# One core, attention and two MoE layers: the small slot's stages put between another slot's products, a third buffer of attention values, the second slot's rows fetched in one step

## The chip, the cores and the metric

The kernel runs on one core of one Trainium2 chip. The metric is the device time of one execution in microseconds (us).

## The reference

```python
def _attn_ref(q, k, v, n_sink, window):
    scores = np.matmul(q, k.transpose(0, 1, 3, 2)) / np.sqrt(D)
    keep = is_sink | in_window
    scores = np.where(keep, scores, -1000000000.0)
    a = np.exp(scores - np.max(scores, axis=-1, keepdims=True))
    a = a / (np.sum(a, axis=-1, keepdims=True) + 1e-09)
    return np.matmul(a, v)

def _moe_ref(x, modality_id, w_gate, modality_bias, w1, w2):
    logits = x @ w_gate + modality_bias[modality_id]
    e_idx = np.argmax(logits, axis=1)
    ...
    for e in range(E):
        mask = e_idx == e
        h = np.maximum(x[mask] @ w1[e], 0.0)
        out[mask] = gate_w[mask, None] * (h @ w2[e])

def _moe2_ref(x, w_in, w_out):
    h = x @ w_in
    g = h * np.clip(h + 3.0, 0.0, 6.0) / 6.0
    return g @ w_out
```

Attention has 4 batches of 8 heads, 768 positions and head size 64; with 4 sink columns and a window of 128. Its output, 3072 tokens of 512, goes through a routed MoE (8 experts, top 1, hidden 1024), and that through a dense layer with a gate (hidden 2048), whose two weights arrive in 64 bits.

## The kernel before

The program is one long schedule, written out by hand: the order in the code is the order on each engine, and each engine (TensorE or PE, VectorE or DVE, ScalarE or ACT, GpSimd or POOL, SyncE or SP) works through its own instructions in that order, waiting for the others by semaphores. SP issues most loads; ACT issues some transfers too; POOL issues the indirect ones. An engine whose next instruction waits holds all that it has behind it.

**Attention** (to about 245 us). `attend(n)` (L1199) lists the pieces of head n beside those of heads n-1 to n-3. At an even n it first issues loads: keys and queries of the pair n+4 (`load_qk`, L204), the values of the pair n itself (`load_v`, L218, buffer `vt`, two buffers), the sink rows of the pair n+2. Those values are read first by `values_mm` (L341) two heads later. `scale_q` (L230) scales the next pair's queries on ACT.

**Routing** (`route`, L377) finds each token's expert; four batches, the last beside the first products of the MoE. Scaled rows go to DRAM (`xs_d`, from ACT, L483), token numbers are scattered into a table `tt_d` (POOL, L488).

**The routed MoE** works in slots (L1419). Slots 0 to 3 are 400 tokens each of the largest expert, slot `SMALL` = 4 holds 128 tokens of another expert with its own weights, slots 5 to 8 are 400 tokens each of the second largest. A slot's token numbers are asked for (`ask`, L1175, `ti`), its rows gathered in four indirect DMAs (`fetch`, `gather`, L718, `xg`), transposed (`slot_x`, L729), multiplied by w1 (`slot_h`, L749: 8 groups of 12 products, L758) and w2 (`slot_y`, L770: 8 half groups of 12, L779), and written (`slot_out`, L848: `yT_d`, `ids_d`, from ACT's queue). After each 12 products stands a `step()` (L1371), which issues what is due: a table `due` says which function runs in which step. A 400 slot has 16 steps, the small slot five. Steps also carry the splits of weights (`weight_split`, L681: ACT copies the high half, POOL or DVE subtracts; pace by `SPLITS`) and the narrowing of the last layer's weights (`narrow`, L866: 32 pieces, each loaded into `cv64`, converted in three sub-steps on ACT, DVE and POOL, stored as `w_d`; pace by `NARROWED`). A load of weights to be split goes into one of three `stg` buffers (`stage`, L670).

**The small slot** has five stages, one function each (L791 to L846): `small_x` transposes the rows, `small_h` makes 8 products of 128x512 per weight half and a ReLU on ACT into `hr`, `small_ht` transposes `hr`, `small_y` makes the second products, `small_yt` transposes back into `ys`. Its weights are used as they are, in fp32 (`raw`, L697; loaded 7 steps ahead by `load_small`, L1159). In the order on PE these stages follow one another between slot 3's last product and slot 5's first; only the transposes of slot 5's rows stand between them.

**The last layer** takes 12 tiles of 256 tokens (from about 585 us). A general path (L1450) for other inputs is in the program and is not entered with these.

The loop over the slots:

```python
for r in range(NS + 1):
    if r == SMALL:
        w = lambda i: W["small"][i]
        h = self.small_h(xT[r]["xT"], w, step)
        h = self.small_ht(h, step)
        y = self.small_y(h, w, step)
        when(pt, lambda y=y, r=r: self.slot_out(self.small_yt(y), tk[r], creg[r]))
    else:
        h = self.slot_h(xT[r]["xT"], weights(r), step)
        y = self.slot_y(h, weights(r), step)
        self.slot_out(y, tk[r], creg[r])
```

Of the kernel before, what the change touches and what calls it, by code (L numbers as in the profile page):

```python
# [54 lines left out]
class Net:  # L55
# [321 lines left out]
    def route(self, b):  # L377
# [107 lines left out]
        def sc(i):  # L485
            n = b * NB + i
            g.memset(self.rt.tile([P, 1], F32, name="apart"), 0.0)
            d = g.indirect_dma_start(out=self.tt, out_offset=IndirectOffsetOnAxis(r["si"][:, i:i + 1], 0),  # L488
                                     in_=self.toki[:, n:n + 1], in_offset=None)
            if not self.looped:  # L490
                self.scattered(d)
# [16 lines left out]
        return q  # L508

# [199 lines left out]
    def tokens(self, base, j=NJ, tp=TP, queue=None):  # L709

        ti = self.gp.tile([tp, j], I32, name=f"ti{j}", bufs=5 if j > 1 else 2)
        d = (queue or self.nc.sync).dma_start(
            out=ti, in_=self.tt[ds(base, j * tp), :].rearrange("(j p) o -> p (j o)", p=tp))
        if not self.looped:
            self.after_scatters(d)
        return ti

    def gather(self, ti, n=NT):  # L718
# [8 lines left out]
        return xg, [lambda i=i: rows(i) for i in range(j)]  # L727

# [62 lines left out]
    def small_x(self, xg):  # L791
# [11 lines left out]
        return r, [turn]  # L803

    def small_h(self, xT, w, side):

        nc = self.nc
        h = self.stg.tile([P, FF], F32, name="hr", tag="stg")
        for z in range(2):
            ph = self.mm.tile([P, 512], F32, name="mm")  # L810
            for k in range(4):
                nc.tensor.matmul(ph, xT[:, k], w(k)[:, z * 512:(z + 1) * 512], start=(k == 0), stop=(k == 3))
            nc.scalar.activation(h[:, z * 512:(z + 1) * 512], ph, AF.Relu)
            side()
        return h

    def small_ht(self, h, side):
        nc = self.nc
        hT = self.hp.tile([P, 8, P], F32, name="h")
        for z in range(2):  # L820
            t = self.mm.tile([P, 512], F32, name="mm").rearrange("p (i q) -> p i q", i=4)
            for i in range(4):
                nc.tensor.transpose(t[:, i], h[:, (4 * z + i) * P:(4 * z + i + 1) * P], self.ident)
            nc.scalar.copy(hT[:, 4 * z:4 * z + 4], t)
            side()
        return hT

    def small_y(self, hT, w, side):
        nc = self.nc
        py = self.mm.tile([P, 512], F32, name="mm")  # L830
        for f in range(8):
            nc.tensor.matmul(py, hT[:, f], w(4 + f // 2)[:, f % 2 * DM:(f % 2 + 1) * DM], start=(f == 0), stop=(f == 7))
            if f == 3:
                side()
        yr = self.yp.tile([P, DM], F32, name="y")
        nc.scalar.copy(yr, py)
        return yr

    def small_yt(self, yr):
        nc = self.nc  # L840
        t = self.pt.tile([P, 4, P], F32, name="tp")
        for d in range(4):
            nc.tensor.transpose(t[:, d], yr[:, d * P:(d + 1) * P], self.ident)
        y = self.stg.tile([P, 4, P], F32, name="ys", tag="stg")
        nc.scalar.copy(y, t)
        return y  # L846
# [19 lines left out]
    def narrow(self, pieces):  # L866
# [16 lines left out]
        def load(i):  # L883
            t = st["t", i] = self.cv.tile([P, 512, 2], I32, name="cv64", bufs=5)
# [28 lines left out]
        at = ((store, 8), (load, -8), (shift, 0), (size, 0), (sign, 1), (rest, 1), (small, 2), (whole, 3))  # L913
        q = [[(f, (k - d) // 3) for f, d in at if (k - d) % 3 == 0] for k in range(-8, 3 * n + 6)]
# [143 lines left out]
    def tile_out(self, g, wo, ids, side=None):  # L1058

        nc = self.nc  # L1060
        for t in range(T2 // P):
# [12 lines left out]
            else:  # L1074
                nc.scalar.copy(o, po)  # L1075
            nc.gpsimd.indirect_dma_start(out=self.out, out_offset=IndirectOffsetOnAxis(ids[:, t:t + 1], 0),  # L1076
# [3 lines left out]
    def build(self):  # L1080
        tc, nc = self.tc, self.nc
        with ExitStack() as ctx:
# [7 lines left out]
            self.w32 = dram.tile([16, P, 1024], F32, name="w32_d")  # L1090
            cp = pool("cp")
# [4 lines left out]
    def fast(self, cp):  # L1096
        tc, nc = self.tc, self.nc
        NBH = B * H
        with ExitStack() as ctx:
# [96 lines left out]
            def turns(s):  # L1196
                return self.small_x(xg[s]) if s == SMALL else self.slot_x(xg[s])

            def attend(n):  # L1199
# [6 lines left out]
                if a and n % 2 == 0:  # L1206
                    self.load_v(n)
# [31 lines left out]
            def scattered(b):  # L1239
# [17 lines left out]
                elif b == 2:  # L1257
                    slow.extend([lambda: self.first_slot(1)])
# [17 lines left out]
            with tc.manual_schedule(engines=COMPUTE):  # L1276
# [38 lines left out]
                def moved():  # L1315
# [3 lines left out]
                    self.cv = pool("cv", 1, cc, **right)  # L1319
                    narrow[:] = self.narrow(self.PIECES)  # L1320
# [22 lines left out]
                begin = [16 * r - 11 * (r > SMALL) for r in range(NS + 2)]  # L1343
# [289 lines left out]
```

## Time and profile before

| | |
|---|---|
| three runs | 1131.01, 1136.57, 1137.31 us; median 1136.57 us |
| the profiled execution | 1140.02 us; span of the profile 1138.2 us |
| granted TensorE clock, mean over the span | 0.986 |
| PE busy | 95% of the span |
| DVE, ACT, POOL busy | 42%, 40%, 23% |
| moved by DMA | 102.09 MB, 90 GB/s in the mean |
| chain that ended last, by engine | PE 78%, DMA 11%, DVE 4%, ACT 2% |

The timeline gives every operation with its start and length; in square brackets stands how long its engine had been idle, and whose work ended that. The span is 1.8 us shorter than the execution's own time, which is 3.5 us above the median of the three runs.

### The profile page before, as it was taken

How to read it: one execution, taken by the hardware profiler on the slowest of the kernel's cores; microseconds unless marked ns; L12 is line 12 of the kernel's file. 1: busy time of each engine (PE TensorE's matmuls, PEld its weight loads, DVE VectorE, ACT ScalarE, POOL GpSimd, SP SyncE). 2: the span in 40 equal slices, each digit the busy share in tenths (PEclk: the TensorE clock that was granted, in tenths of full speed). 3: DMA queues.
4: the chain of work that ended last, by engine and by line, in shares of the span. 5: the costliest groups of instructions: out<-in, count | busy, mean ns of one | idle time of the engine just before them, and what ended most of it. 6: DMA issues, size and time to landing. Idle time of an engine off the chain costs nothing.

```text
span 1138.2 us, 18251 instructions
## 1 busy us (share of the span) xinstructions
PE 1086.2 (95%) x6805; PEld 993.7 (87%) x6805; DVE 480.8 (42%) x1271; ACT 454.5 (40%) x1111; POOL 257.8 (23%) x458
## 2 busy tenths in 40 slices
PE   9999989897999979999999999999999999999995
PEld 6998878796999947999997989989989889899894
DVE  6666748655544414552243413314224134133140
ACT  4565636443355535652253413314224234143140
POOL 3433616445144324442031000000000000000000
PEclk9999989999999998999999999999999999999998
DMA  6343866514697795756332110100100101000000
GB/s 178 102 128 98 144 127 160 116 58 95 209 198 200 192 311 136 232 137 114 66 104 83 29 33 5 38 17 22 38 10 29 37 10 29 21 18 20 11 10 22
DMA packets 59891, 102.09 MB, mean 90 GB/s; under 512 B 17552, under 2 KB 34576, under 8 KB 59792
## 3 DMA queue, kind: packets, MB, share of 16 engines
q1 hardware_dynamic: 39966, 74.16, 25.3%
q10 hardware_dynamic: 13986, 13.53, 4.6%
q0 software_dynamic: 5840, 13.13, 4.5%
q8 instruction: 56, 0.92, 0.4%
q14 instruction: 43, 0.35, 0.1%
HBM read 72.87 MB, written 27.92 MB: 89 GB/s over the span
## 4 chain that ended last, share of the span: by engine, by line
PE 78%; DMA 11%; DVE 4%; ACT 2%; issue 1%; POOL 1%; SPq 1%; ACTq 0%; POOLq 0%; DVEq 0%
PE mm L1067 23%; PE mm L1045 22%; PE mm L779 10%; PE mm L758 9%; PE s L247 5%; PE o L354 2%; PE o L353 2%; DMA vt<-vv 2%; DMA yT_d<-y 1%; DMA xg<-xs_d,ti 1%; PE tp L318 1%; DMA ti<-tt_d 1%; DMA w<-w 1%; DMA stg<-w 1%; DMA ids_d<-ti 1%
## 5 line engine op out<-in xcount | busy, mean ns | idle before, releaser
L1045 PEld LDWEIGHTS mm<-yh,w 128*128 128x128 f32 x2304 | 274.6, 189 | 3.3 <-DVE u L1050 2.5
L1045 PE MATMUL mm<-yh,w 128*128 128x256 f32 x2304 | 275.1, 281 | 2.3 <-DVE u L1050 2.3
L1067 PE MATMUL mm<-w,ga 128*128 128x512 f32 x936 | 220.6, 394 | 0.1
L1067 PEld LDWEIGHTS mm<-w,ga 128*128 128x128 f32 x936 | 175.2, 188 | 39.9 <-DVE u L1050 0.3
L1048 ACT ACTIVATE r<-mm,b 128x256 f32<-128x256 f32 x192 | 91.2, 475 | 247.1 <-PE mm L1045 246.6
L779 PE MATMUL mm<-h,w 128*128 128x400 f32 x768 | 149.9, 350 | 3.2 <-DVE h L761 3.1
L758 PE MATMUL mm<-xT,w 128*128 128x400 f32 x768 | 143.5, 346 | 0.0
L779 PEld LDWEIGHTS mm<-h,w 128*128 128x128 f32 x768 | 139.4, 190 | 4.2 <-DVE h L761 4.2
L758 PEld LDWEIGHTS mm<-xT,w 128*128 128x128 f32 x768 | 139.8, 188 | 0.5 <-issue 0.5
L1050 DVE SCALAR_TENSOR_TENSOR u<-r,mm 128x256 f32<-128x256 f32 x192 | 80.8, 421 | 139.6 <-ACT r L1048 139.2
L1076 POOL DMA_INDIRECT out_dram<-ot,idt x24 | 23.1, 962 | 491.4 <-ACT ot L1075 368.9
L1073 DVE COPY ot<-mm 128x512 f32<-128x512 f32 x12 | 8.3, 692 | 222.0 <-PE mm L1067 222.0
L247 PE MATMUL s<-kz,qq 128*128 128x260 f32 (+1 forms) x384 | 95.6, 372 | 1.7 <-ACT qq L233 1.2
L283 ACT ACTIVATE pr<-s,mn 128x132 f32<-128x132 f32 x160 | 52.4, 370 | 75.8 <-DVE mn L272 40.5
L688 POOL TENSOR_TENSOR w<-stg,w 128x512 fp32r<-128x512 f32 x35 | 48.0, 1376 | 144.8 <-ACT w L686 134.1
L247 PEld LDWEIGHTS s<-kz,qq 128*128 128x128 f32 x384 | 62.5, 192 | 7.1 <-ACT qq L233 1.7
L761 DVE SCALAR_TENSOR_TENSOR h<-mm,h 128x400 fp32r<-128x400 f32 x64 | 36.5, 572 | 74.3 <-ACT h L760 73.2
L1035 DVE SCALAR_TENSOR_TENSOR ga<-u,ga 128x256 fp32r<-128x256 f32 x156 | 67.1, 430 | 0.0
L1034 ACT ACTIVATE ga<-u 128x256 fp32r<-128x256 f32 x156 | 63.8, 409 | 1.1 <-DVE u L1050 1.1
L354 PE MATMUL o<-vt,pt5p 128*128 128x66 f32 x320 | 62.6, 278 | 0.0
L353 PE MATMUL o<-vt,pt5d 128*128 128x66 f32 x320 | 61.4, 274 | 0.0
L336 POOL TENSOR_SCALAR_AFFINE_SELECT pt5d<-pt6a 128x256 f32<-128x256 f32 x64 | 30.5, 477 | 130.5 <-ACT pt6a L333 130.3
(228 smaller groups left out, 1249.8 us busy)
## 6 DMA issues: line engine op xcount, KB each, us to landing
stg<-w SPq DMA_DIRECT2D x16, 512.0 KB
cv<-w_in SPq DMA_DIRECT2D x16, 512.0 KB
w_d<-cva SPq DMA_DIRECT2D x32, 256.0 KB
cv<-w_out SPq DMA_DIRECT2D x16, 512.0 KB
stg<-w_d SPq DMA_DIRECT2D x16, 512.0 KB
yT_d<-y ACTq DMA_DIRECT2D x8, 800.0 KB
vt<-vv SPq DMA_DIRECT2D x16, 396.0 KB
kz<-kE SPq DMA_DIRECT2D x32, 197.0 KB
```

The lines of the kernel that those rows point to most:

```text
L247: nc.tensor.matmul(s[:, a, :n], q[:, b], k[:, c:c + n], start=True, stop=True)
L283: self.nc.scalar.activation(pr[:, i], s[:, a, P:P + W], AF.Exp, bias=mn[:, i:i + 1], scale=-1.0)
L353: mm(o[:, j], d[:, j - 1], vt[:, j], start=False, stop=False)
L354: mm(o[:, j], p[:, j - 1], vt[:, j - 1], start=False, stop=False)
L758: nc.tensor.matmul(ph[:, :T1], w(k)[:, wi, c], xT[:, xi, k], start=(n == 0), stop=(n == 11))
L779: nc.tensor.matmul(py[:, :T1], wf[:, wi], h[:, hi, f], start=(n == 0), stop=(n == 23))
L1034: nc.scalar.mul(g(0, f), u, 1.0 / 6.0)
L1035: nc.vector.scalar_tensor_tensor(g(1, f), u, 1.0 / 6.0, g(0, f).bitcast(F32), ALU.mult, ALU.subtract)
L1045: nc.tensor.matmul(ph[:, :T2], w, yh[:, b, k], start=(n == 0), stop=(n == 11))
L1048: nc.scalar.activation(r, ph[:, :T2], AF.Relu, bias=self.b3)
L1050: nc.vector.scalar_tensor_tensor(u, r, 6.0, ph[:, :T2], ALU.min, ALU.mult)
L1067: nc.tensor.matmul(po, g(a, f)[:, t * P:(t + 1) * P], w[:, b], start=(n == 0), stop=(n == 47))
```

## The change

- The five functions of the small slot become one, `small_slot`, which returns its stages by step number. They are due in steps 57 (in slot 3's second products) and 64 to 76 (in slot 5's). The small slot has no steps of its own any more, so that every later step number falls by five. `xs4`, `hT` and `ys` sit in the `stg` buffers, `hr` and `yr` in a new pool `sm` of one buffer.
- Slot 5's token numbers, rows and transposes come in steps 45, 48 and 59, all beside slot 3; before, in steps 50, 53 and 65, the transposes between the small slot's stages.
- To make room, `cv64` has four buffers instead of five, and a piece's load is listed five sub-steps ahead of its use instead of eight. The knots of `SPLITS` and `NARROWED` move with the step numbers.
- `vt` has three buffers; `attend(n)` issues the values of pair n+2 instead of those of pair n. At the start, the first pair's values and the small inputs are issued ahead of the second pair's keys and queries.
- Slot 1: its token numbers are asked for in attention's list (`scattered(2)`) right behind `first_slot(1)`, which runs at once; its four gathers are issued in one step instead of four.
- The general path has loops of single-row transfers in place of indirect DMAs (`spread`, `gather_rows`), with three new DRAM tensors. It is not entered here; its diff is left out.

```diff
-SPLITS = ((4, 0), (8, 8), (20, 8), (56, 16), (65, 16), (74, 24), (80, 24), (100, 32), (106, 32), (116, 40),
-          (126, 40), (133, 48), (134, 48), (148, 56))
-NARROWED = 105
+SPLITS = ((4, 0), (8, 8), (20, 8), (56, 16), (63, 16), (71, 24), (78, 24), (96, 32), (101, 32), (111, 40),
+          (121, 40), (128, 48), (129, 48), (143, 56))
+NARROWED = 100
...
-        vt = self.vp.tile([P, 2, NB, DV], F32, name="vt")
+        vt = self.vp.tile([P, 2, NB, DV], F32, name="vt", bufs=3)
...
-    def small_x(self, xg):
...
+    def small_slot(self, x, w, out):
...
         def turn():
             t = self.pt.tile([P, 4, P], F32, name="tp")
             for k in range(4):
-                nc.tensor.transpose(t[:, k], xg[:, 0, k * P:(k + 1) * P], self.ident)
-            r["xT"] = self.xtp.tile([P, 4, P], F32, name="xT")
+                nc.tensor.transpose(t[:, k], x()[:, 0, k * P:(k + 1) * P], self.ident)
+            r["xT"] = self.stg.tile([P, 4, P], F32, name="xs4", tag="stg")
             nc.scalar.copy(r["xT"], t)
...
+        def hidden(z):
+            if z == 0:
+                r["h"] = self.sm.tile([P, FF], F32, name="hr", tag="sm")
             ph = self.mm.tile([P, 512], F32, name="mm")
             for k in range(4):
...
+                nc.tensor.matmul(ph, r["xT"][:, k], w(k)[:, z * 512:(z + 1) * 512], start=(k == 0), stop=(k == 3))
+            nc.scalar.activation(r["h"][:, z * 512:(z + 1) * 512], ph, AF.Relu)
+
+        def turned(z):
+            if z == 0:
+                r["hT"] = self.stg.tile([P, 8, P], F32, name="hT", tag="stg")
             t = self.mm.tile([P, 512], F32, name="mm").rearrange("p (i q) -> p i q", i=4)
...
+        def outer(z):
+            if z == 0:
+                r["py"] = self.mm.tile([P, 512], F32, name="mm")
+            for f in range(4 * z, 4 * z + 4):
+                nc.tensor.matmul(r["py"], r["hT"][:, f], w(4 + f // 2)[:, f % 2 * DM:(f % 2 + 1) * DM],
+                                 start=(f == 0), stop=(f == 7))
...
+        def back():
...
+            out(y)
+
+        return {57: turn, 64: lambda: hidden(0), 65: lambda: hidden(1), 69: lambda: turned(0),
+                70: lambda: turned(1), 73: lambda: outer(0), 74: lambda: outer(1), 76: back}
...
-            t = st["t", i] = self.cv.tile([P, 512, 2], I32, name="cv64", bufs=5)
+            t = st["t", i] = self.cv.tile([P, 512, 2], I32, name="cv64", bufs=4)
...
-        at = ((store, 8), (load, -8), (shift, 0), (size, 0), (sign, 1), (rest, 1), (small, 2), (whole, 3))
+        at = ((store, 8), (load, -5), (shift, 0), (size, 0), (sign, 1), (rest, 1), (small, 2), (whole, 3))
...
-                if a and n % 2 == 0:
-                    self.load_v(n)
+                if n % 2 == 0 and n + 2 < NBH:
+                    self.load_v(n + 2)
...
-                    slow.extend([lambda: self.first_slot(1)])
+                    self.first_slot(1)
+                    slow.extend([None, None, lambda: ask(1)])
...
-                self.load_qk(2)
                 self.load_sink(0)
                 self.consts(cp, tmp)
                 ready = self.mask_kind(cp, tmp) + self.route_inputs(cp, tmp)
+                self.load_v(0)
+                self.load_qk(2)
...
-                begin = [16 * r - 11 * (r > SMALL) for r in range(NS + 2)]
+                begin = [16 * (r - (r > SMALL)) for r in range(NS + 2)]
...
-                        when(pt, *fetch(r))
-                    when(t - (1 if r == 1 else 3), lambda: ask(r))
+                        got = fetch(r)
+                        when(pt, *([lambda: [f() for f in got]] if r == 1 else got))
+                    if r != 1:
+                        when(t - 3, lambda: ask(r))
...
+                    if r > SMALL:
+                        b = begin[r] - 16
                     if r != 2:
-                        arrive(r, EARLY if r == 1 else begin[r - 2] + 5 if r == SMALL + 1 else b)
-                    turned(r, b + 1 if r == SMALL + 1 else b + 11)
+                        arrive(r, EARLY if r == 1 else b)
+                    if r != SMALL:
+                        turned(r, b + 11)
                 when(when_small, load_small)
+                ssteps = self.small_slot(lambda: xg[SMALL], lambda i: W["small"][i],
+                                         lambda y: self.slot_out(y, tk[SMALL], creg[SMALL]))
+                for t, f in ssteps.items():
+                    when(t, f)
```

What the compiled order shows at two places. A row is one engine's line, operation, output <- inputs and size, with a count where it repeats.

On PE, from slot 3's last products to slot 5's second; L779 and L758 are the 400 token slots' products, L812 and L832 the small slot's, L823 and L843 its transposes, L740 those of slot 5's rows. Before:

```order
L779 MATMUL mm<-h,w 128x400 x48
L812 MATMUL mm<-w,xT 128x512 x8
L740 MATMUL tp<-ident,xg 128x100 x4
L823 MATMUL mm<-ident,hr 128x128 x4
L740 MATMUL tp<-ident,xg 128x100 x4
L823 MATMUL mm<-ident,hr 128x128 x4
L740 MATMUL tp<-ident,xg 128x100 x4
L832 MATMUL mm<-w,h 128x512 x4
L740 MATMUL tp<-ident,xg 128x100 x4
L832 MATMUL mm<-w,h 128x512 x4
L758 MATMUL mm<-xT,w 128x400 x12
L843 MATMUL tp<-ident,y 128x128 x4
```

And now, where the same lines are L803, L782, L833, L848, L841 and L857:

```order
L803 MATMUL mm<-h,w 128x400 x12
L782 MATMUL mm<-xT,w 128x400 x12
L833 MATMUL mm<-w,xs_4913 128x512 x4
L782 MATMUL mm<-xT,w 128x400 x12
L833 MATMUL mm<-w,xs_4913 128x512 x4
L782 MATMUL mm<-xT,w 128x400 x48
L841 MATMUL mm<-ident,hr 128x128 x4
L782 MATMUL mm<-xT,w 128x400 x12
L841 MATMUL mm<-ident,hr 128x128 x4
L782 MATMUL mm<-xT,w 128x400 x12
L803 MATMUL mm<-h,w 128x400 x24
L848 MATMUL mm<-w,hT 128x512 x4
```

Between two stages of the small slot stand now 12 to 48 products of slot 5, where before there were four transposes or nothing.

On POOL, around the four gathers of slot 1's rows (L688 is a weight split's subtraction, L724 a gather, L487 and L488 belong to a scatter). Before:

```order
L688 TENSOR_TENSOR w<-stg,w 128x512 x4
L414 MEMSET r_ohz 128x8
L724 DMA xg<-xs_d,ti_3435 100x512
L688 TENSOR_TENSOR w<-stg,w 128x512
L724 DMA xg<-xs_d,ti_3435 100x512 x3
L487 MEMSET apart 128x1
L488 DMA tt_d<-toki,r_si 26624x1
```

And now, where L701 is the subtraction and L736 the gather:

```order
L701 TENSOR_TENSOR w<-stg,w 128x512 x4
L414 MEMSET r_ohz 128x8
L736 DMA xg<-xs_d,ti_3438 100x512 x4
L701 TENSOR_TENSOR w<-stg,w 128x512
L493 MEMSET apart 128x1
L494 DMA tt_d<-toki,r_si 26624x1
```

Three gathers moved ahead of one subtraction, and that subtraction behind them.

## Rows read from the trace of the kernel before

**Rows 1.** Page, part 1: TensorE (busy us, share, instructions)

```profile
PE 1086.2 (95%) x6805; PEld 993.7 (87%) x6805; DVE 480.8 (42%) x1271; ACT 454.5 (40%) x1111; POOL 257.8 (23%) x458
```

**Rows 2.** Timeline, SyncE queue, 138 to 145 us (start us, us, engine, line)

```profile
138.86 0.48 SPq L221 DMA_DIRECT2D vt<-vv  x1
```

**Rows 3.** Timeline, TensorE, 143 to 168 us ([idle before <- releaser])

```profile
143.77 0.71 PE L247 MATMUL s<-kz,qq 128*128 128x128 f32 x3
...
151.97 0.83 PE L247 MATMUL s<-kz,qq 128*128 128x128 f32 x4
...
159.78 0.62 PE L351 MATMUL o<-vt,pt6a 128*128 128x66 f32 x2 [5.33 <-DMA vt<-vv]
...
167.79 0.82 PE L247 MATMUL s<-kz,qq 128*128 128x128 f32 x4
```

**Rows 4.** Timeline, ScalarE, same stretch

```profile
157.59 0.84 ACT L233 ACTIVATE qq<-qq 128x768 f32<-128x768 f32 x1 [2.68 <-DMA qq<-qT]
```

**Rows 5.** Timeline, GpSimd, 263 to 273 us

```profile
267.87 1.27 POOL L688 TENSOR_TENSOR w<-stg,w 128x512 fp32r<-128x512 f32 x1 [0.62 <-ACT w L686]
...
270.67 1.00 POOL L724 DMA_INDIRECT xg<-xs_d,ti  x1 [0.30 <-issue]
271.97 1.00 POOL L724 DMA_INDIRECT xg<-xs_d,ti  x1 [0.30 <-issue]
```

**Rows 6.** Timeline, TensorE, 268 to 287 us

```profile
268.17 2.48 PE L779 MATMUL mm<-h,w 128*128 128x400 f32 x12
...
275.13 0.43 PE L740 MATMUL tp<-ident,xg 100*128 100x100 f32 x3
283.11 0.43 PE L740 MATMUL tp<-ident,xg 100*128 100x100 f32 x1 [7.54 <-DMA xg<-xs_d,ti]
283.24 3.73 PE L779 MATMUL mm<-h,w 128*128 128x400 f32 x12
```

**Rows 7.** Timeline, ScalarE and its queue, 271 to 285 us

```profile
271.16 0.33 ACTq L483 DMA_DIRECT2D xs_d<-xs  x1
...
283.95 0.72 ACT L476 ACTIVATE xs<-xb,r_gt 128x512 f32<-128x512 f32 x1 [7.81 <-DMA xs_d<-xs]
```

**Rows 8.** Stretches of 5 us: each engine busy, clock, DMA share, GB/s

```profile
275.00:280.00 5.00, 0.57 (x5) 0.36 (x3) 0.97 (x2) 0.72 (x1) 4.23 (x9) 0.93 1.00 178
```

**Rows 9.** Timeline, GpSimd and SyncE queue, 390 to 399 us

```profile
390.62 1.01 POOL L724 DMA_INDIRECT xg<-xs_d,ti  x1 [12.02 <-PE mm L779]
...
393.57 4.61 SPq L704 DMA_DIRECT2D w<-w  x8
```

**Rows 10.** Timeline, TensorE, 394 to 437 us

```profile
394.33 8.99 PE L779 MATMUL mm<-h,w 128*128 128x400 f32 x48
403.16 2.74 PE L812 MATMUL mm<-w,xT 128*128 128x512 f32 x6
406.11 4.56 PE L812 MATMUL mm<-w,xT 128*128 128x512 f32 x10 [0.21 <-DMA w<-w]
...
414.61 0.66 PE L823 MATMUL mm<-ident,hr 128*128 128x128 f32 x4 [3.59 <-ACT hr L813]
...
426.55 0.93 PE L740 MATMUL tp<-ident,xg 100*128 100x100 f32 x4 [4.62 <-DVE xT L743]
...
435.94 0.60 PE L843 MATMUL tp<-ident,y 128*128 128x128 f32 x4
```

**Rows 11.** Timeline, ScalarE and TensorE, 451 to 459 us

```profile
451.75 0.62 ACT L686 CAST w<-stg 128x512 fp32r<-128x512 f32 x1 [7.89 <-DMA stg<-w]
...
454.13 4.59 PE L779 MATMUL mm<-h,w 128*128 128x400 f32 x22 [2.22 <-DVE h L761]
```

**Rows 12.** Loads of cv: SyncE queue, ScalarE; last row: tile cv, first and last start

```profile
298.26 3.64 SPq L885 DMA_DIRECT2D cv<-w_in  x5
...
306.45 0.67 ACT L895 ACTIVATE cvm<-cv 128x512 f32<-128x512 f32 x1 [0.26 <-DMA cv<-w_in]
...
L895 ACT ACTIVATE cvm<-cv x32: 657/670/695, 306.5 to 498.5; 128x512 f32<-128x512 f32 x32
```

More of the change, by code (lines that the diff above doesn't have):

```diff
@@ L486, in sc @@
             n = b * NB + i
+            if self.looped:
+                nc.sync.dma_start(out=self.sid[i * P:(i + 1) * P, :], in_=r["si"][:, i:i + 1])
+                if i == NB - 1:
+                    self.spread(self.sid, S, E * NT, lambda to, k: nc.sync.dma_start(
+                        out=self.tt[ds(to, 1), :], in_=self.tokd[ds(k + b * S if b else k, 1), :]))
+                return
             g.memset(self.rt.tile([P, 1], F32, name="apart"), 0.0)
@@ L489, in sc @@
                                      in_=self.toki[:, n:n + 1], in_offset=None)
-            if not self.looped:
-                self.scattered(d)
+            self.scattered(d)
         on = lambda f, *a: (lambda: f(*a))
@@ L508, in route, with spread @@
         return q
+    def spread(self, places, n, most, move):
+        nc = self.nc
+        row = self.ix.tile([1, n], I32, name="row")
+        nc.sync.dma_start(out=row, in_=places.rearrange("n o -> o n"))
+        with self.tc.For_i(0, n, 1) as k:
+            move(nc.sync.value_load(row[0:1, ds(k, 1)], min_val=0, max_val=most - 1), k)
     def scattered(self, inst):
@@ L826, in small_ht @@
[L826 to L846, printed above, removed]
+                nc.tensor.transpose(t[:, i], r["h"][:, (4 * z + i) * P:(4 * z + i + 1) * P], self.ident)
@@ new lines, in back @@
+        def back():
+            t = self.pt.tile([P, 4, P], F32, name="tp")
+            for d in range(4):
+                nc.tensor.transpose(t[:, d], r["y"][:, d * P:(d + 1) * P], self.ident)
+            y = self.stg.tile([P, 4, P], F32, name="ys", tag="stg")
+            nc.scalar.copy(y, t)
+            out(y)
+        return {57: turn, 64: lambda: hidden(0), 65: lambda: hidden(1), 69: lambda: turned(0),
+                70: lambda: turned(1), 73: lambda: outer(0), 74: lambda: outer(1), 76: back}
@@ L1196, in turns @@
             def turns(s):
-                return self.small_x(xg[s]) if s == SMALL else self.slot_x(xg[s])
+                return self.slot_x(xg[s])
             def attend(n):
@@ L1319, in moved @@
                     self.cv = pool("cv", 1, cc, **right)
+                    self.sm = pool("sm", 1, cc, **right)
                     narrow[:] = self.narrow(self.PIECES)
@@ L1419, in fast @@
                 for r in range(NS + 1):
-                    if r == SMALL:
-                        w = lambda i: W["small"][i]
-                        h = self.small_h(xT[r]["xT"], w, step)
-                        h = self.small_ht(h, step)
-                        y = self.small_y(h, w, step)
-                        when(pt, lambda y=y, r=r: self.slot_out(self.small_yt(y), tk[r], creg[r]))
-                    else:
+                    if r != SMALL:
                         h = self.slot_h(xT[r]["xT"], weights(r), step)
@@ L1533, in dense @@
             v.memset(self.tab["cnt"], 0.0)
+            nc.sync.dma_start(out=self.tokd.rearrange("(n p) o -> p (n o)", p=P), in_=self.toki)
             for b in range(B):
@@ L1563, in more_slots @@
                         c = nc.scalar.value_load(at[2 + m], min_val=0, max_val=NT)
-                        ti = self.tokens(base + m * T1 if m else base)
-                        xg, rows = self.gather(ti)
+                        xg, ti = self.gather_rows(base + m * T1 if m else base)
                         xT, turn = self.slot_x(xg)
-                        for f in rows + turn:
+                        for f in turn:
                             f()
```

55 lines of the change are left out of this document (30 added, 25 removed).

## The prediction

> **What bounds the kernel now.** I read the page's busy shares first, then the waits of TensorE (PE), then the timeline around each of the long ones. PE is busy for 1086.2 us, 95% of the span [rows 1], so this is a PE kernel, and only two things can shorten it: less work on PE, of which the change removes none, or shorter pauses. The span is 1138.2 us, so PE's pauses hold 52 us in all, and four places hold most of what an edit of order can touch. At each, the bracket of the row tells which work ended the pause. Around 155 us PE stood 5.33 us for attention values [rows 3]; around 276 us, 7.54 us for a gather [rows 6]; between 406 and 430 us it stood three times, 0.21 for weights, 3.59 for ScalarE (ACT) and 4.62 for VectorE (DVE) [rows 10]; at 454 us, 2.22 us for DVE [rows 11]. A pause costs more than its bracket, since the products behind it are slower for a few microseconds: twelve took 2.48 us before the gather's pause and 3.73 us after it [rows 6].
>
> The sum is made against the profiled execution, 1140.0 us, which is 3.5 us above the median of 1136.6; I carry the difference over to the median unchanged.
>
> **Values, third buffer.** The load of `vt` was issued at 138.86 us [rows 2], and PE had it at 159.78 us, 20.9 us later [rows 3]; three weight loads and the pair's queries stand ahead of it in SyncE's (SP's) order. The new order issues this pair's values one pair, about 15 us, earlier, and the load that stands at 138.86 us now is wanted by the next pair. What the pause cost: the same scores product stood at 143.77 us in one head, at 151.97 us in the next, at 167.79 us in the one with the pause [rows 3]. Pitches are 8.2 and 15.8 us, so 7.6 us were lost. Late next are the queries of the same queue: ACT waited for them until 157.59 us [rows 4], and its next exponentials come some 2 us later than PE would want to reuse their buffer, at about 160 us; that is within a few tenths. I take **-7.5 us**, bounds -8.3 (with a little more from the clock) and -1 (the queries' wait moves onto PE in full).
>
> **The start.** The second pair's loads go behind the first pair's values and the small inputs. Less stands beside the first queries, and the second pair's may come late. The trace shows neither; the nearest pauses are those of about 1.3 us for first queries, so I take **0**, bounds -1.2 and +1.5.
>
> **Second slot's rows.** PE did three of four transposes at 275.13 us and waited until 283.11 us for the last [rows 6]. The last gather was issued at 271.97 us and took 11 us; the third, issued at 270.67 us, had landed by 275.1 us, in 4.4 us at most [rows 5, 6]. Between the two stands ACT's first row write to `xs_d`, at 271.16 us [rows 7]; then the DMA engines were full, with only 178 GB/s moved [rows 8]. In the new order the second gather stands where the subtraction of 267.87 us stood, and the others follow it at 1.3 us each [rows 5], so that the last is issued at about 270.3 us, ahead of all those writes, and I take it to land like the third. Paid for that: this subtraction, of 1.27 us [rows 5], now runs after the fourth, to about 272.7 us. Its weight half is the last one that the products from 268.17 us use, near their end at about 270.3 us [rows 6]; PE waits some 2.4 us there, anew. Then all four transposes run at about 275.1 + 2.4 and are done by 278 instead of 283.5 us, 5.5 us and more won, of which ACT may take back a part: its own pause until 283.95 us [rows 7] is for a row write to land, which nothing here shortens, and the copies of the transposed rows are behind it. **-4.5 us**, bounds -6 and 0.
>
> [...]
>
> **Small slot.** This is the largest term. Slot 3's products end at 403.16 us; the last of the small slot's stages, L843, ends at 435.94 + 0.60 = 436.5 us, with slot 5's first twelve products in between: 33.4 us [rows 10]. What PE has to do there: 32 passes of 128x512 (the L812 and L832 products; 10 passes took 4.56 us [rows 10], so 0.456 each), 14.6 us; 12 small transposes, about 1.7 us; slot 5's 16 transposes, about 1.6 us, which move but stay; twelve products of slot 5 at 8.99/4 = 2.25 us [rows 10]. That is 20.1 us, and 13.3 us are pauses and slow clock. Woven in, each stage finds its input ready, since at least 12 products of slot 5 stand between it and the one before [the order rows], longer than ACT's copy. The stages add no work. Their operations on ACT are the same four copies and two ReLUs.
>
> Two inputs can be late. The small weights were issued from 393.57 us [rows 9] and one was still awaited at 406.11 us, 12.5 us on [rows 10]; their buffers are free once slot 3's first products end, which is two times 8.99 us before 403.16 us [rows 10], at about 385 us. In SP's order a store of narrowed weights stands ahead of them, which waits for POOL, and POOL stood 12.02 us before its gather at 390.62 us [rows 9]. The bracket names PE there; by the code that gather waits for slot 5's token numbers, too, and these are now asked for five steps earlier. So I expect the weights by about 400 us, against 405.4 us when they are wanted. If they are no earlier than before, PE stands up to 4 us. And ACT's queue may again stand at slot 3's end behind a transfer. I take **-13 us**, bounds -13.3 and -6.
>
> **Behind it.** At 451.75 us ACT had waited 7.89 us for a weight load, and DVE, late for that reason, kept PE 2.22 us [rows 11]; with the slow clock behind it I count 3.1. That load's buffer held `ys` of the small slot. Now it waits for other things (a subtraction, and PE's reading of `xs4`), both long done by then: **-3.1 us**, bounds -3.3 and +4 (a new wait of the same kind, as long as the small slot's 3.59 or 4.62).
>
> **One buffer fewer for narrowing.** I cost it at nothing: ACT hardly waited for these loads, 0.26 us at the first [rows 12]. Their cover is the time a buffer takes to come round. That is the last rival below.
>
> The general path's new loops are not entered. All else is the same work: no cost.
>
> **Sum:** 0 - 7.5 - 4.5 - 13 - 3.1 = -28.1 us. The profiled execution would be 1111.9 us, the median **1108.5 us**.
>
> **The rivals.**
>
> A. *The transfers' bytes set the landings, not their order.* In the gather's stretch the DMA engines were full, and if they were so at the other places, queries or weights take the place of the values, the gather gains its 1.8 us only, the wait at 454 us stays, and the small weights are as late as before. For it: [rows 8], and the queries' wait [rows 4]. Against: both the values and the small weights are wanted later than issued by more than any landing seen, 20.9 us or less. Time: values halfway between their bounds, -4.6, gather -1.8, small slot -9, behind it 0: -15.4, **1121 us**.
>
> B. *ACT at the ends of the slots.* The outputs leave from ACT's queue, and the 3.59 us of [rows 10] were ACT standing behind such a transfer. If that stays at slot 3's end, slot 5's first products run out of result buffers, which the small slot's stages now share, and half of the small slot's term is given back: -28.1 + 7, and up to 4 more behind it: **1117 to 1120 us**.
>
> C. *Slower: four buffers starve the narrowing.* A buffer of `cv64` holds a piece while it lands and for two of its three sub-steps. Pieces follow one another every (498.5 - 306.5)/31 = 6.2 us [rows 12], about 5.7 us after the change. Five buffers came round in 31 us, four do in 22.8 us; less two thirds of a piece, 3.8 us, a load may take 19 us. Beyond that every piece is late by a quarter of the excess, and ACT, which has the products' ReLUs behind it, holds PE. The first load was there after 8.2 us [rows 12]; with 20.9 us, the values' landing, 32 x 1.9/4 = 15 us are lost; at 22.5 us the gain is gone, from 23.2 us on the kernel is slower. At 25 us: 32 x 6/4 = 48 us, **1156 us**. Against it: the mean of 90 GB/s, and the small weights, which landed within some 12.5 us of the first issue [rows 9, 10].
>
> D. *It does nothing*: if the fills of one pause reappear in full in the next, about **1136 us**.
>
> **How the numbers follow.** The forecast has 0.55, A 0.2, B 0.14, C 0.06, D 0.05. All bounds at their best give -32.1 (1104.5, and some 5 less if the runs fall like the lowest of the three shown); A with a further 5 us, a new wait in the small slot's place, gives 1126. The range **1099 to 1127** leaves out C, D and edges of the others, about 0.18. A difference of 0.5% (5.7 us) is what a measurement of this kernel can tell from none. Faster by more: the forecast, A and B, less a little, 0.88; within it: 0.06; slower: 0.06.
>
> **What would show it.** No wait of PE for `vt` near 155 us, and equal pitches of the heads there. A wait of some 2 us for the weight subtraction in slot 0's second products, and no 7 us one for the gather. In slot 5's first products the L833 and L841 rows start without brackets, and PE's busy share between slot 3's end and slot 5's end is above 95%. The small weights' loads are issued before 390 us. If PE waits there for ACT's ReLU, B is right; if ACT waits for `cv` loads, C; if PE waits for the weights or the queries, A. PE's busy time itself should fall a little, by the slow products behind the pauses, and nothing else.

## The result, and the profile after

The changed kernel took 1122.53 us in the median of four runs (1118.72 to 1123.28), the kernel before 1134.64 us in four (1131.01 to 1137.31): a ratio of 0.9889, 95% interval 0.9849 to 0.9928. That is 12 us less, where 28 us less were forecast. The time lies in the range given, but only because the range was drawn to take in the rivals A and B. Timed again in a later job (experiment `e7_after`, eleven runs), the ratio was 0.9938 (0.9910 to 0.9965), about 7 us.

The profiled execution of the changed kernel took 1122.69 us, its span is 1120.9 us. PE's row of the page, which answers to [rows 1]:

```profile
PE 1080.5 (96%) x6805; PEld 991.4 (88%) x6805; DVE 484.4 (43%) x1271; ACT 454.6 (41%) x1111; POOL 257.9 (23%) x458
```

PE's busy time fell by 5.7 us (the products behind pauses, as foreseen) and its idle time from 52.0 to 40.4 us. What it waits for now, from the waits of PE in the changed kernel (engine, operation, line, releaser: us in total, times, longest):

```profile
PE mm L782 <- ACT hT L842: 3.5, 1, 3.5
PE mm L1062 <- DVE u L1067: 3.0, 1, 3.0
PE s L247 <- ACT pr L283: 2.6, 3, 2.2
PE tp L764 <- DMA xg<-xs_d,ti: 2.3, 2, 1.4
PE mm L803 <- POOL apart L493: 2.2, 1, 2.2
PE mm L841 <- DVE h L785: 2.1, 1, 2.1
```

The 5.33 us for values [rows 3], the 7.54 us for the gather [rows 6] and the 3.59 and 4.62 us in the small slot [rows 10] are gone. New are 3.5 us for `hT`, 2.1 us in slot 5's first products, 2.2 us behind the gathers, and 2.2 us near the start.

Where the time went is read best from the first product of each stage on PE (from the timelines; us):

| stage begins | before | after | after less before |
|---|---|---|---|
| slot 0, first products | 235.7 | 229.5 | -6.2 |
| slot 1, first products | 294.5 | 283.9 | -10.6 |
| slot 1, second products | 312.1 | 303.4 | -8.7 |
| slot 3, second products | 385.2 | 376.4 | -8.9 |
| slot 6, first products | 474.7 | 454.9 | -19.8 |
| slot 7, first products | 511.1 | 494.1 | -17.0 |
| first tile | 582.7 | 565.7 | -17.0 |
| first tile, second products | 608.1 | 593.0 | -15.1 |

Attention gave 6.2 us, the second slot 2.5 net, small slot and slot 5 together 11, and 4.7 us were lost again behind them. From there to the last tile the difference stays at -15.2; the rest of the spans' 17.3 us is the tail behind the last product.

**The start.** Timelines of ScalarE and of TensorE in the changed kernel:

```profile
13.94 0.84 ACT L233 ACTIVATE qq<-qq 128x768 f32<-128x768 f32 x1 [3.45 <-DMA qq<-qT]
```

```profile
15.36 0.93 PE L247 MATMUL s<-kz,qq 128*128 128x128 f32 x4 [2.19 <-ACT pr L283]
```

The second pair's queries, now behind the first values and the small inputs, were scaled 3.2 us later than before (at 13.94 for 10.76 us), and PE stood 2.19 us. The heads were 2.1 us late from there on.

**Second slot.** Timelines of GpSimd and of TensorE, which answer to [rows 5] and [rows 6]:

```profile
264.88 1.01 POOL L736 DMA_INDIRECT xg<-xs_d,ti  x1 [0.30 <-issue]
265.92 1.27 POOL L701 TENSOR_TENSOR w<-stg,w 128x512 fp32r<-128x512 f32 x1
```

```profile
267.24 0.49 PE L803 MATMUL mm<-h,w 128*128 128x400 f32 x1 [2.17 <-POOL apart L493]
...
273.69 0.51 PE L764 MATMUL tp<-ident,xg 100*128 100x100 f32 x4
...
283.93 9.08 PE L782 MATMUL mm<-xT,w 128*128 128x400 f32 x48
294.47 9.07 PE L782 MATMUL mm<-xT,w 128*128 128x400 f32 x48 [1.46 <-DVE h L785]
```

All four gathers had landed when the transposes came up at 273.69 us, without a bracket. The wait of 2.17 us stands under the name of the memset that follows the subtraction at 265.92 us, and is the one foreseen (2.4 us). At 294.47 us PE then stood 1.46 us: ACT, and DVE behind it, were held at the queue for slot 0's outputs.

**Small slot.** Timelines of TensorE, SyncE's queue and ScalarE, which answer to [rows 9] and [rows 10]:

```profile
395.80 2.34 PE L782 MATMUL mm<-xT,w 128*128 128x400 f32 x12
397.98 3.60 PE L833 MATMUL mm<-w,xs 128*128 128x512 f32 x8
...
406.63 9.35 PE L782 MATMUL mm<-xT,w 128*128 128x400 f32 x48
415.82 0.60 PE L841 MATMUL mm<-ident,hr 128*128 128x128 f32 x4
...
420.69 0.75 PE L841 MATMUL mm<-ident,hr 128*128 128x128 f32 x4 [2.08 <-DVE h L785]
424.96 3.79 PE L782 MATMUL mm<-xT,w 128*128 128x400 f32 x12 [3.53 <-ACT hT L842]
```

```profile
376.03 10.12 SPq L717 DMA_DIRECT2D w<-w  x8
...
404.60 3.02 SPq L687 DMA_DIRECT2D stg<-w  x2
```

```profile
401.34 0.33 ACTq L870 DMA_DIRECT2D ids_d<-ti  x1
...
418.35 0.62 ACT L699 CAST w<-stg 128x512 fp32r<-128x512 f32 x1 [6.23 <-DMA stg<-w]
...
424.32 0.58 ACT L842 COPY hT<-mm 128x512 f32<-128x512 f32 x1 [2.82 <-POOL w L701]
```

The small weights were issued from 376 us on instead of 393.57, and no product of the small slot waits for them. But of two weight loads, issued from 404.60 us on, the first was not there until 418.35 us, 13.7 us later; ACT stood 6.23 us for it, with the ReLUs behind it, and PE 2.08 and 3.53 us. So the stages' own waits are gone, and a load took their place. The 3.53 us came by way of the buffers: the change put `hT` into a `stg` buffer, and its copy waited 2.82 us for the subtraction of the late weights, which by the code frees one. PE's busy share between slot 3's end and slot 5's end, for which the prediction gave over 95% as a sign, was 90% (53.49 of 59.10 us; columns as below):

```profile
395.80:454.90 59.10, 53.49 (x254) 44.93 (x254) 19.39 (x31) 26.91 (x61) 19.81 (x17) 0.94 0.71 192
```

It was not for want of bandwidth: in the 5 us before 405 us the DMA engines, at a share of 1.02, moved 397 GB/s. Two stretches of 5 us (columns: length; PE, PEld, DVE, ACT, POOL busy; clock, DMA share, GB/s):

```profile
405.00:410.00 5.00, 5.00 (x23) 3.80 (x22) 0.31 (x2) 2.34 (x6) 2.33 (x3) 1.00 1.03 101
410.00:415.00 5.00, 5.00 (x29) 5.00 (x28) 3.03 (x5) 2.12 (x5) 3.46 (x3) 1.00 0.98 54
```

Here they were busy to the full, too, and moved 101, then 54 GB/s. These stretches lie behind ACT's `ids_d` at 401.34 us: a slot's 400 token numbers, written to DRAM one by one, 4 bytes each.

### The profile page after: what moved, and what is told of

Same layout as the page of the kernel before. It is cut to its first block, busy times and chain, and to the rows that moved or that the text cites. A ratio compares the mean times of both kernels' runs of the same rounds, so it can differ in the third digit from the quotient of the medians.

```text
span 1120.9 us, 18250 instructions
## 1 busy us (share of the span) xinstructions
PE 1080.5 (96%) x6805; PEld 991.4 (88%) x6805; DVE 484.4 (43%) x1271; ACT 454.6 (41%) x1111; POOL 257.9 (23%) x458
## 4 chain that ended last, share of the span: by engine, by line
PE 83%; DMA 6%; DVE 4%; issue 2%; ACT 2%; POOL 1%; SPq 0%; ACTq 0%; POOLq 0%; DVEq 0%
PE mm L1062 24%; PE mm L1084 24%; PE mm L803 9%; PE mm L782 9%; PE s L247 6%; PE o L354 3%; PE o L353 3%; PE tp L318 1%; DMA xg<-xs_d,ti 1%; DMA stg<-w 1%; DMA cv<-w_out 1%; DMA qq<-qT 1%; DMA yT_d<-ys 1%; PE tp L393 1%; PE tp L764 1%
## 5 line engine op out<-in xcount | busy, mean ns | idle before, releaser
L803 PE MATMUL mm<-h,w 128*128 128x400 f32 x768 | 151.8, 351 | 2.2 <-POOL apart L493 2.2
L782 PE MATMUL mm<-xT,w 128*128 128x400 f32 x768 | 146.1, 349 | 5.0 <-ACT hT L842 3.5
L782 PEld LDWEIGHTS mm<-xT,w 128*128 128x128 f32 x768 | 140.7, 190 | 7.0 <-ACT hT L842 3.9
L803 PEld LDWEIGHTS mm<-h,w 128*128 128x128 f32 x768 | 139.4, 190 | 3.6 <-POOL apart L493 2.5
L701 POOL TENSOR_TENSOR w<-stg,w 128x512 fp32r<-128x512 f32 x35 | 47.8, 1370 | 138.6 <-ACT w L699 123.1
L784 ACT ACTIVATE h<-mm 128x400 fp32r<-128x400 f32 x64 | 31.9, 504 | 72.9 <-PE mm L782 57.6
```

The lines of the kernel that those rows point to most:

```text
L782: nc.tensor.matmul(ph[:, :T1], w(k)[:, wi, c], xT[:, xi, k], start=(n == 0), stop=(n == 11))
L803: nc.tensor.matmul(py[:, :T1], wf[:, wi], h[:, hi, f], start=(n == 0), stop=(n == 23))
```

## The experiments

The two theories after the result: **S**, the 4-byte writes at a slot's end keep the DRAM reads behind them waiting, and these late loads make most of the pauses around the small slot, wherever it stands; **C**, the change's own price, four `cv64` buffers, holds ACT. On the chips of the three jobs, the kernel before had medians of 1122.39 us (20 runs; e1, e2, e3, e5), 1131.53 us (22 runs; e4, e6, e7, e8) and 1131.45 us (11 runs; e9 to e11), so only ratios, and times within one job, are compared.

**e1_ids.** The token numbers go from the table to `ids_d` as one row:

```diff
-        nc.scalar.dma_start(out=self.ids[ds(c, n), :].rearrange("(j p) o -> p (j o)", p=p), in_=ti)
...
+            d = nc.scalar.dma_start(out=self.ids[ds(c, n), :].rearrange("n o -> o n"),
+                                    in_=self.tt[ds(frm, n), :].rearrange("n o -> o n"))
+            self.after_scatters(d)
...
```

> The changed kernel, with a slot's token numbers written to ids_d from the table tt_d as one contiguous row (DRAM to DRAM) in place of 400 single numbers of 4 bytes from SBUF. Theory S (the 4-byte writes keep DRAM reads behind them waiting): after slot 3 the weight loads stg<-w land within 8 us instead of 13.7, ScalarE's 6.2 us wait for them falls under 2 us, TensorE's waits of 2.1 and 3.5 us in slot 5's first products go, and so does the 2.3 us wait for a gather near 482 us; slot 5's second products start at least 6 us earlier counted from slot 3's end, the time is 7 to 13 us below the changed kernel's 1122.5, about 1111. Theory C (four cv64 buffers are the cause): nothing of this moves, 1121 to 1124.

1107.36 us (1106.43 to 1112.20), ratio 0.9873 (0.9826 to 0.9920). Its waits of PE, and the same two stretches:

```profile
PE mm L803 <- POOL apart L493: 2.1, 1, 2.1
...
PE mm L782 <- DVE h L785: 1.2, 1, 1.2
PE mm L782 <- ACT hT L842: 0.9, 1, 0.9
PE tp L764 <- DMA xg<-xs_d,ti: 0.7, 1, 0.7
```

```profile
405.00:410.00 5.00, 5.00 (x29) 5.00 (x28) 2.17 (x3) 4.49 (x11) 3.54 (x3) 1.00 0.51 164
410.00:415.00 5.00, 5.00 (x30) 4.96 (x30) 3.70 (x5) 3.25 (x7) 4.49 (x5) 1.00 0.98 292
```

The waits for `hT` and in slot 5's first products fell to 0.9 and 1.2 us, the 2.3 us for gathers to 0.7, and the 3 us in the first tile are gone. From slot 5's first to its second products it takes 26.4 us (393.7 to 420.1) in place of 32.8 (395.8 to 428.6). Against the changed kernel's ratio of 0.9938, from another chip, 0.9873 is 7 us less, the lower end of what S expected; the two intervals just overlap, and the changed kernel was not timed on this chip, so that the time is settled by e8, e9 and e10 below. The same stretches move 164 and 292 GB/s. S holds for these waits. How long single packets took shows it directly, in the trace's packet records: stretches with five or more packets of over 1.2 us, from 300 us on (first to last, us, and their number):

```
before    314-321 (21)  338-348 (50)  375-382 (28)  420-425 (34)  444-448 (23)  481-489 (38)  518-527 (52) ...
after     309-311 (12)  321-327 (6)   331-340 (46)  368-374 (28)  406-416 (49)  459-459 (9)  469-476 (31)  502-510 (36) ...
e1_ids    331-332 (5)
e8, e9, e11    none
e10_ids4  305-312 (39)  330-335 (21)  350-351 (5)  370-373 (16)  405-410 (30)  456-463 (40)  495-503 (33)  531-536 (21) ...
```

In the changed kernel's stretch from 406 us on the slowest, packets of 2048 bytes as these weight loads have, took up to 4.0 us each. `ti` is still read from the table in 400 pieces of 4 bytes in e1_ids, and leaves no such stretch: it is the writes to DRAM.

**e10_ids4.** Control: the fast version (e8 below), with the copy from DRAM to DRAM in 400 pieces of 4 bytes:

```diff
-            ... out=self.ids[ds(c, n), :].rearrange("n o -> o n"), in_=self.tt[ds(frm, n), :].rearrange("n o -> o n"))
+            ... out=self.ids[ds(c, n), :].rearrange("(j p) o -> p (j o)", p=p),
+                in_=self.tt[ds(frm, n), :].rearrange("(j p) o -> p (j o)", p=p))
```

> The fast version (contiguous write, second pair's loads first), with the token numbers still copied from DRAM to DRAM, but as 400 pieces of 4 bytes again. If 4-byte writes to DRAM make what follows wait, the slow packets behind each slot's end are back and the time is near that of the changed kernel without its start loss, 9 to 14 us above the fast version. If the source in SBUF, or the wait for it on ScalarE, was what mattered, nothing comes back: within 2 us of the fast version.

1117.09 us (1114.85 to 1120.75), ratio 0.9873 (0.9823 to 0.9923). The slow stretches are back (above), and so is the full share with little moved:

```profile
405.00:410.00 5.00, 5.00 (x28) 4.76 (x27) 1.69 (x3) 3.98 (x10) 3.04 (x3) 1.00 1.14 70
```

That is 7.6 us above e11_best of the same job, which has one edit more. Against the fast version's ratio of 0.9788, from another chip, it is 0.0085 of 1131 us more, 9.6 us; the two intervals do not overlap. So it is the small pieces, not the source in SBUF.

**e2_cv4.** The kernel before with `bufs=4` for `cv64` and `(load, -5)`.

> The kernel before, with cv64 at four buffers and loads five sub-steps ahead, nothing else. Theory S: no cost, within 2 us of before (about 1135). Theory C: ScalarE waits for cv loads by 5 us or more in all, and the time is 5 to 10 us above before.

1123.39 us, ratio 1.0012 (0.9986 to 1.0039): no cost. ACT's waits between 295 and 500 us do hold one for such a load:

```profile
ACT w L686 <- DMA stg<-w: 7.0, 1, 7.0
...
ACT cvm L895 <- DMA cv<-w_out: 5.3, 1, 5.3
```

The 5.3 us are what C asked for, and the time did not follow. In the changed kernel ACT's waits for such loads are 5.4 us in all; but e1_ids, with four buffers too, has lost the waits that C was to explain. C falls.

**e9_before_ids.** The kernel before with e1's edit and nothing of the change.

> The kernel before with the contiguous write of the token numbers alone: the small slot in its own place, two vt buffers, the second slot as it was. If the late loads, not the order, made most of the small slot's pauses in the kernel before, this edit alone takes most of them: 10 us or more below before (ratio 0.990 or less), slot 5's first products at most 24 us after the small slot's start (29 and more until now). If the order made them, as the prediction said, 3 to 6 us below before, and the small slot still takes 28 us.

1114.16 us (1113.06 to 1116.57), ratio 0.9833 (0.9785 to 0.9881): this edit alone, timed beside the kernel before on one chip, brings 17 us. The whole change brought 7 us in the later job, where the intervals are apart, and 12 us in the first, where they overlap. The small slot in its own place, timeline of TensorE:

```profile
399.06 7.03 PE L812 MATMUL mm<-w,xT 128*128 128x512 f32 x16
...
406.27 0.60 PE L823 MATMUL mm<-ident,hr 128*128 128x128 f32 x4
...
413.59 3.70 PE L832 MATMUL mm<-w,h 128*128 128x512 f32 x8 [0.50 <-ACT h L824]
416.73 2.75 PE L758 MATMUL mm<-xT,w 128*128 128x400 f32 x12
```

From its first product at 399.06 us to slot 5's at 416.73 us it takes 17.7 us: 7.03 us for the first 16 passes, in one run, and two pauses of half a microsecond. From slot 3's second products to slot 6's first, the profiles have 84.0 us before (e6), 77.9 with the change (e7), 73.0 here and 72.2 with both (e8). Woven in or not, the small slot costs its own work once nothing is late; weaving is worth 0.8 us then, in these profiles.

All thirteen profiles of this document divide in the same way. The four with the one-row write (e1, e8, e9, e11) take 72.1 to 73.0 us there, and 22.6 us from the first tile's first products to its second. The nine others take 75.3 to 89.5 and 25.1 to 29.4 us, whatever the order and the chip. Among the nine the order shows less than the landings do: e5_vt, with the small slot and the writes of before, took 78.2 us, and the changed kernel 78.5 and 77.9.

One pause of the kernel before does not fit S. Timeline of ScalarE in its first profile:

```profile
413.59 0.32 ACTq L853 DMA_DIRECT2D ids_d<-ti  x1
413.96 0.60 ACT L813 ACTIVATE hr<-mm 128x512 f32<-128x512 f32 x1 [10.71 <-DMA cv<-w_out]
```

Slot 3's token numbers were issued at 413.59 us, when PE's 3.59 us for this ReLU [rows 10] were all but over, and between 407 and 412 us the DMA engines had moved 394 GB/s. The 4.62 us lie behind that issue, the 3.59 us do not; what held ACT before it is open.

**e6_before and e7_after.** The two kernels unchanged, on one chip.

> The kernel before, unchanged, profiled once more. If the 5.3 us wait for vt belongs to the kernel, it is there again near 155 us, with the first slot's products at about 235 us. If it belonged to the one execution (the kernel of two runs ago with the same attention showed no such wait and had its first slot at 226.8 us), it is absent, the first slot starts at about 227 us and the span is about 1121.

> The changed kernel, unchanged, timed beside the kernel before on one chip. With the wait for vt in the kernel before: 12 us below it, as measured first. Without it, the sum over the stages of the runs so far is -2.5 (second slot) -7.6 (small slot and what follows) +1.9 (start) = -8 us, a ratio of about 0.993. The first wait of the second pair's scores (2.2 us near 15 us) and the 3.5 us wait for hT are there again.

The kernel before: 1133.23 us, with this row for the values:

```profile
155.00 0.41 PE L351 MATMUL o<-vt,pt6a 128*128 128x66 f32 x2 [0.61 <-DMA vt<-vv]
```

0.61 us in place of 5.33 [rows 3], and the first slot at 227.5 us in place of 235.7. The same attention in e2_cv4 showed no such wait, in e9_before_ids this one:

```profile
PE o L351 <- DMA vt<-vv: 2.2, 1, 2.2
```

So the wait differs from profile to profile: 5.3, 2.2, 0.6 and 0 us. Each is from another job or another version, so that execution and chip can't be told apart. The landing goes with a stretch that looks like those above. While the load was under way, from 140 to 145 us, the DMA engines moved 77 GB/s in the first profile and 71 in e9_before_ids, 137 in e6_before and 127 in e2_cv4, at a share of 0.90 to 1.03; the first and the last of these:

```profile
140.00:145.00 5.00, 4.92 (x38) 4.21 (x37) 2.65 (x7) 2.39 (x8) 1.58 (x5) 1.00 0.98 77
140.00:145.00 5.00, 5.00 (x39) 4.33 (x38) 2.53 (x5) 2.52 (x8) 1.58 (x5) 1.00 1.03 127
```

The routing's scatters, writes of 4 bytes as well, were issued just ahead, from 122 to 136 us. That they made the values late is likely from this, and was not tried.

The changed kernel: 1123.33 us (1117.61 to 1127.03), ratio 0.9938, as the second half of the expectation had it. Its first slot starts 1.2 us later than in e6_before, its slot 1 5.7 us earlier, slot 6 10.0 us earlier, and the first tile's second products 10.4 us earlier.

**e5_vt.** The kernel before with `bufs=3` for `vt` and `load_v(n + 2)`, the first pair's values issued behind the small inputs.

> The kernel before, with three vt buffers and the values issued a pair earlier, the start left as it was. The 5.3 us wait for vt goes. By the prediction's term the MoE's first slot starts 7.5 us earlier and the time is 6 to 8 us below before, about 1127; if the queries' wait or later pauses take it back, 0 to 3 us below.

1121.36 us, ratio 0.9999 (0.9975 to 1.0023): no gain on this chip, where the attention of before showed no such wait (e2_cv4). The first slot starts at 226.7 us here and at 226.8 us there. What the third buffer is worth on a chip or in an execution with the wait was not timed by itself.

**e3_start.** The changed kernel with `self.load_qk(2)` ahead of the sink rows again.

> The changed kernel, with the second pair's keys and queries issued first again at the start. Theory S and C alike: the scores of the first heads are 2 us earlier from 15 us on. If pauses further on absorb the loss, as the trace of the changed kernel suggests (its lead of -6.2 us at the first slot with -8.7 at the values), 0 to 2 us below the changed kernel, 1120.5 to 1122.5.

1111.99 us (1110.34 to 1114.07), ratio 0.9906 (0.9872 to 0.9939). Its first slot starts at 226.7 us, in e1_ids, which has the change's start, at 228.6: 1.9 us that nothing absorbs here. The changed kernel itself was not timed in this job; against its 0.9938 from another, 0.9906 is 3.6 us less, with intervals that overlap.

**e4_gather.** The changed kernel with the gathers in four steps:

```diff
-                        when(pt, *([lambda: [f() for f in got]] if r == 1 else got))
+                        when(pt, *got)
```

> The changed kernel, with the second slot's four gathers in four steps again (three of them behind one weight subtraction). Theory of the prediction: the 2.2 us wait for that subtraction goes, and a wait of 5 to 8 us for the last gather comes back; slot 1 starts 3 us later than in the changed kernel, the time is 2 to 4 us above it. Rival: the token numbers, which are asked for earlier in any case, made the gain; then no wait for the gather comes back and the time is 2 us below the changed kernel.

1125.84 us, 2.5 us above the changed kernel of the same job; the intervals of the ratios overlap (0.9926 to 0.9989 here, 0.9910 to 0.9965 there), so that the trace has to decide. TensorE's timeline:

```profile
269.86 0.42 PE L764 MATMUL tp<-ident,xg 100*128 100x100 f32 x3
276.21 0.43 PE L764 MATMUL tp<-ident,xg 100*128 100x100 f32 x1 [5.92 <-issue]
```

The wait for the last gather is back, 5.92 us (named "issue"), and slot 1 starts 4.5 us later from slot 0's second products on. The order of the gathers made the gain, not the earlier question for token numbers.

**e8_ids_start and e11_best.** e1's and e3's edits together; and with them the subtraction behind the gathers done by DVE.

> The changed kernel with both edits, the contiguous write of the token numbers and the second pair's loads first again. The two act at different places, so their gains add: 2 us from the start and 4 to 8 us from the writes below the changed kernel, and 14 us or more below the kernel before (ratio at or under 0.987). If the start's loss is absorbed further on, as at first, the write's gain alone.

> The fast version, with the one subtraction that the change moved behind the four gathers done on VectorE. TensorE's 2.1 to 2.4 us wait for it goes; ScalarE's row writes are still as late, so 0.5 to 2.5 us below the fast version. If VectorE is late for the routing instead, 0 to 2 us above it.

e8_ids_start: 1106.41 us (1103.90 to 1108.51), ratio 0.9788 (0.9756 to 0.9820), 17 us below the changed kernel of the same job and faster than both kernels by more than the intervals. Its waits of PE:

```profile
PE mm L803 <- POOL apart L493: 2.4, 1, 2.4
PE s L247 <- ACT qq L233: 2.4, 1, 2.4
...
PE mm L782 <- ACT hT L842: 0.9, 1, 0.9
PE tp L764 <- DMA xg<-xs_d,ti: 0.7, 1, 0.7
```

e11_best: 1109.45 us, ratio 0.9803 (0.9765 to 0.9842) on another chip, no better. The 2.4 us for the subtraction went, but in its profile ACT stood for its row writes and PE behind it (timelines of ScalarE and TensorE):

```profile
270.48 0.72 ACT L476 ACTIVATE xs<-xb,r_gt 128x512 f32<-128x512 f32 x1 [6.45 <-DMA xs_d<-xs]
...
275.33 0.72 ACT L476 ACTIVATE xs<-xb,r_gt 128x512 f32<-128x512 f32 x1 [4.12 <-DMA xs_d<-xs]
```

```profile
277.61 0.93 PE L764 MATMUL tp<-ident,xg 100*128 100x100 f32 x4 [4.34 <-DVE xT L767]
```

These writes share a stretch with the scatters, which are 4-byte writes too; that these hold them is likely from their place and was not tried.

## Why the prediction was right or wrong

- **What the sum stands on.** "I carry the difference over to the median unchanged" was the first step that failed. The profiled execution of before was 5.4 us above the median of its four runs, and what I priced in it, the values' wait above all, was not there in the same size in other profiles. The two spans differ by 17.3 us, the medians by 12.1.
- **Values, -7.5.** The mechanism is right for that one execution: the heads went from 2.1 us late to 6.6 us early there, 8.7 us, a little more than the bound of -8.3. (The row at 143.77 us is the second of its four products; the first stood at 143.66, so the pitches were 8.3 and 15.8 us.) Wrong as a term of the kernel: the wait was 5.3, 0.6, 0 and 2.2 us in four profiles of the same attention, and e5_vt has no gain. The rows showed one landing; nothing in them said that it would land so late again.
- **The start, 0.** Mis-sized: +2.1 us at the heads, +1.2 to +1.9 us at the first slot, outside the bound of +1.5. I took the first queries' waits as the nearest row, and counted no queue behind the moved loads.
- **Second slot, -4.5.** Right in mechanism, and near in price: -4.4 us in the first pair of profiles from slot 0's first products to slot 1's and 1.9 given back by ACT, 2.5 net; -6.9 and 1.8 given back on one chip, 5.1 net; the new wait was 2.2 us for 2.4 forecast. Issued ahead of the row writes, the last gather took 8.8 us at most to land, and 6.1 us in e11_best (262.10 to 268.20); issued behind the first of them it took 11 us in the kernel before and 9.9 us in e4 (266.29 to 276.21). The Trainium skill ("DMA: Bandwidth & Descriptors", "Issuing engines are not separate DMA queues") says that transfers started by ScalarE, SyncE and GpSimd run on the same 16 engines and interleave. No run here tests that sharing by itself; the difference here came with the order of issue.
- **Small slot and behind it, -16.1.** Mis-sized, and for a wrong reason; this is the step that cost most. In the first pair it gave 11 us, on one chip 6.1. The step that failed is "13.3 us are pauses and slow clock. Woven in, each stage finds its input ready": the pauses were put down to the order of the stages, and the runs show that late landings made most of them (e9_before_ids: 73.0 us with the order kept, where e6_before has 84.0; the profiles are from two chips, and e5_vt's 78.2 us says how far one profile can lie from another). The 3.59 us before the ReLU stay open. The small weights did come in time, as forecast. And "Now it waits for other things [...], both long done by then" looked at when the load is issued, not at how long it takes: 13.7 us. The new wait that I had as a bound, +4, came, with 5.6 us on PE.
- **One buffer fewer, 0.** Right (e2_cv4).
- **Behind slot 5.** Not in the sum: 2.8 us for a gather in slot 6 and 1.9 us in the first tile, both late landings again, both gone in e1_ids.
- **The rivals.** A came nearest in time (1121) and in kind, landings decide and not order, with a wrong cause: where the loads were late, the bytes were few. Its 1.8 us for the gather are about what the earlier issue is worth, 271.97 less some 270.3 us. B does not hold: no wait of PE for ACT's ReLU stands at slot 3's end. Its sum has a slip, too: -28.1 + 7 is 1115.5 us, not 1117. The Trainium skill ("DMA: Bandwidth & Descriptors", "Specifications") says that transfers under 512 bytes are read, modified and written. The runs agree that small writes are dear (9.6 us for the token numbers of the nine slots), and show that others' reads waited behind them; the reading and modifying itself no run here shows.

## What to carry to other kernels

A wait for a DMA has two parts, when it could be issued and how long it took to land; before an order is changed for it, look at the second, and price it from more than one profiled execution. Full DMA engines with little moved were the sign here: then find who writes in small pieces. Here one line, 400 numbers as one row instead of 400 writes, was worth more than the reordering of a stage, and left 0.8 us for that reordering to gain.

## What was not expected of the hardware

- In the changed kernel slot 3's 400 writes of 4 bytes (1.6 KB) were followed by 10 us, 406 to 416, in which loads' packets took up to 4.0 us and the engines, busy to the full, moved 54 to 101 GB/s; as one row, the same bytes left no such stretch (five slow packets within 1 us in e1_ids, none in three other profiles).
- The spread of the runs may go with it: on one chip the kernel before took 1127.02 to 1139.47 us (11 runs), and with the one-row write alone 1113.06 to 1116.57 us (e9_before_ids). Four runs are too few to say how much.
